# Retention attention and a multiplicative FFN: the first weight quarter in Strassen order, a new order of loads, and q of units 0 and 1 scaled by VectorE

**Chip, cores, metric.** One core of one Trainium2 chip. The metric is the device time of the slowest (here the only) core, in microseconds (us). The kernels of one round ran on the same chip.

## The reference

```python
scores = q @ k.T / sqrt(64);  D[i, j] = gamma_h ** (i - j) for i >= j, else 0
x = ((scores * D) @ v), heads side by side        # 8 batches x 576 tokens, 8 heads x 64 -> 4608 x 512
a = x @ w1;  b = x @ w2                           # 512 x 1024 each
out = ((a * b) @ w3) @ w_out                      # 1024 x 1024, 1024 x 512
```

q, k, v are float32. The weights come as float64 and are read as pairs of 32-bit words; the kernel turns them into float32 itself.

## The kernel before

It works in units of up to 128 positions of two batches (unit 0 has 64). In a unit TensorE transposes k and q, makes scores and a running state, and forms x ("pv"). The products with w1 and w2 ("up") use Strassen's scheme, seven products for eight, one quarter of the features at a time. A weight block of 128 x 512 pairs is converted by VectorE and ScalarE: VectorE cuts out exponent and mantissa (`begin_block`), ScalarE clamps the exponent in two steps, VectorE joins them (`end_block`). The head of the program interleaves all this by hand. Every engine follows its own instructions in the order written here.

```python
    def strassen_weights(fp):
        tt("S1", "A21", "A22", ALU.add)
        tt("S2", "S1", "A11", ALU.subtract)
        yield
        tt("S3", "A11", "A21", ALU.subtract)
        tt("S4", "A12", "S2", ALU.subtract)
        live["S", fp] = True
        yield
...
    def conversion():            # a generator; convert(n) takes n of its steps, convert_up_to(n) ends n blocks
        yield from begin_block()
        while converted[0] < len(blocks):
            if begun[0] < len(blocks) and converted[0] not in (1, 2, 3):
                yield from begin_block()      # the next block is begun before this one is ended
            yield from end_block()
            if begun[0] == converted[0] < len(blocks):
                yield from begin_block()
...
        c = ffn.tile([P, 4, 2, TB], F32, tag="c", name="c", bufs=1)       # in up(), one quarter
        p1 = product(None, "A11", "B11")
        nc.scalar.copy(c[:, 0], p1)
        if first:
            product(p1, "A12", "B21")          # adds into the same bank: waits for the copy
            aside.pop(0)()
        plus(product(None, "S2", "T2"), 1, 0)  # plus: an addition on VectorE and two conversion steps
        plus(product(None, "S3", "T3"), 2, 1)
...
    load_block()                 # the head of the program; load(unit, what)
    load(0, "v")
    load_block()
    load(1, "kq")
    load_block()
    load(1, "v")
    load_block()
    scale(0, "q")                # GpSimd
    front(0, "k"); keep_busy(4); front(0, "q")      # transposes; idle products that keep TensorE at work
    convert(3)
    score(0); scale(0, "v"); state(0)
    convert_up_to(1)
    pv(0)
    load(2, "kqv"); load_block(); load_block()
    convert_up_to(2)
    load_block()
    scale(1, "q")                # GpSimd
    front(1, "k"); keep_busy(6); front(1, "q")
    convert(3)
    scale(1, "v"); score(1); state(1)
    convert_up_to(3); load_block(); convert_up_to(4)
    first_sums = strassen_weights(0); next(first_sums)
    pv(1)
    ...
    up(0, 0, 0, conv=2, tail=False, first=True)
```

## Time and profile before

| | before |
|---|---|
| time, median of 5 runs | 859.64 us (858.93 to 861.71) |
| span of the profiled run | 857.7 us |
| TensorE (PE) / VectorE (DVE) / ScalarE (ACT) / GpSimd (POOL) busy | 98 / 56 / 21 / 14 % |
| first up product starts | 30.57 us |
| TensorE gapless from unit 3's q on | 49.58 to 94 us |

The lines behind these numbers stand in the prediction. One view is added: the chain of work that ended last begins, followed back, in the middle of the head (columns: start us, us, what).

```profile
49.54 0.04 issue
49.58 1.09 PE tp L237 x8
```

What happens before 49.54 counts only as far as it moves that point or one after it.

### The profile page before, as it was taken

The page shows a single profiled execution, that of the slowest core. Times are in us where ns is not written, and L with a number is a line of the kernel's source. Part 1 is how long each engine was busy: PE and PEld are TensorE (multiplying, and loading weights), DVE is VectorE, ACT ScalarE, POOL GpSimd, SP SyncE. Part 2 cuts the span into 40 slices and gives each one's busy share as a digit, 9 for nine tenths or more (in the row PEclk, how much of TensorE's full clock was granted, in tenths as well). Part 3 has the DMA queues.
Part 4 walks back from the last instruction along what each step waited for, and adds up shares of the span by engine and source line. Part 5 has one row for each costly group of instructions (what it writes and reads, how often), then busy time and mean ns, then how long its engine had stood idle before and what let it go on. Part 6 is the DMA issues. An engine that isn't in the chain of part 4 may idle for free.

```text
span 857.7 us, 15368 instructions
## 1 busy us (share of the span) xinstructions
PE 844.7 (98%) x6293; PEld 770.5 (90%) x6293; DVE 482.6 (56%) x797; ACT 179.1 (21%) x358; POOL 119.7 (14%) x96
## 2 busy tenths in 40 slices
PE   8989999999999999999999999999999999999998
PEld 7889999644888999999999999999999999999996
DVE  4899998996744444454544544544454434335343
ACT  3666343342121111010111010111010201001000
POOL 3010020001212213221221130203030101000000
PEclk9999999999999999999999999999999999999999
DMA  9994453454246525352542171534140000000001
GB/s 195 218 225 114 100 96 103 114 156 70 42 98 125 98 34 87 62 109 47 87 86 38 27 122 31 95 65 60 31 69 25 2 25 1 26 25 1 25 1 50
DMA packets 213879, 64.01 MB, mean 75 GB/s; under 512 B 195752, under 2 KB 204200, under 8 KB 213808
## 3 DMA queue, kind: packets, MB, share of 16 engines
q1 hardware_dynamic: 167376, 43.33, 26.4%
q10 hardware_dynamic: 46432, 19.70, 10.3%
q8 instruction: 49, 0.80, 0.4%
q14 instruction: 22, 0.18, 0.1%
HBM read 53.55 MB, written 9.44 MB: 73 GB/s over the span
## 4 chain that ended last, share of the span: by engine, by line
PE 88%; DVE 4%; issue 1%; ACT 1%; DMA 0%; ACTq 0%; DVEq 0%
PE up L506 46%; PE po L617 25%; PE ps L461 6%; PE xps L309 4%; PE sc L252 4%; PE xps L302 2%; PE st L274 1%; DVE c L511 1%; PE tp L237 1%; DMA out_dram<-ot 0%; DVE e L400 0%; ACT e L389 0%; DVE w L411 0%; DVE ab L537 0%; DVE wS L169 0%
## 5 line engine op out<-in xcount | busy, mean ns | idle before, releaser
L511 DVE TENSOR_TENSOR c<-up,c 128x384 f32<-128x384 f32 x240 | 132.5, 552 | 175.2 <-PE up L506 170.9
L506 PE MATMUL up<-xT,wA 128*128 128x192 f32 x1152 | 212.5, 328 | 0.6 <-ACT c L519 0.6
L506 PEld LDWEIGHTS up<-xT,wA 128*128 128x128 f32 x1152 | 190.5, 190 | 3.9 <-ACT c L519 0.9
L506 PE MATMUL up<-T,wS 128*128 128x192 f32 x768 | 140.6, 326 | 0.0
L506 PEld LDWEIGHTS up<-T,wS 128*128 128x128 f32 x768 | 127.4, 190 | 0.2 <-issue 0.2
L617 PE MATMUL po<-w3o,ab 128*128 128x256 f32 x456 | 104.0, 380 | 0.3 <-ACT ot L639 0.3
L617 PEld LDWEIGHTS po<-w3o,ab 128*128 128x128 f32 x456 | 86.0, 190 | 12.1 <-ACT ot L639 0.7
L621 DVE TENSOR_TENSOR ot<-po,ot 128x256 f32<-128x256 f32 x90 | 38.0, 423 | 69.5 <-PE po L617 66.6
L506 PE MATMUL up<-xT,wS 128*128 128x192 f32 x384 | 70.6, 327 | 0.6 <-DVE c L511 0.5
L255 DVE TENSOR_TENSOR pm<-sc,mask 128x512 f32<-128x512 f32 (+1 forms) x80 | 45.4, 627 | 45.4 <-PE sc L252 45.4
L506 PE MATMUL up<-T,wA 128*128 128x192 f32 x384 | 70.2, 326 | 0.0
L531 ACT COPY c<-up 128x384 f32<-128x384 f32 x48 | 22.9, 478 | 226.0 <-PE up L506 224.1
L223 POOL TENSOR_TENSOR ld_v<-ld_v,gk 128x1024 f32<-128x1024 f32 (+1 forms) x17 | 34.5, 2030 | 242.3 <-DMA ld_v<-in_v_dram 179.6
L617 PE MATMUL po<-wB,forms 128*128 128x256 f32 x288 | 65.3, 379 | 0.0
L506 PEld LDWEIGHTS up<-xT,wS 128*128 128x128 f32 x384 | 63.6, 190 | 1.4 <-DVE c L511 1.4
L506 PEld LDWEIGHTS up<-T,wA 128*128 128x128 f32 x384 | 63.7, 190 | 0.0
L617 PEld LDWEIGHTS po<-wB,forms 128*128 128x128 f32 x288 | 54.6, 190 | 7.7 <-issue 0.3
L461 PE MATMUL ps<-wo,w3T 128*128 128x512 f32 x128 | 55.4, 593 | 1.3 <-DVE w3T L415 1.3
L461 PEld LDWEIGHTS ps<-wo,w3T 128*128 128x128 f32 x128 | 23.9, 190 | 32.2 <-issue 30.5
L537 DVE TENSOR_TENSOR ab<-c 128x768 f32<-128x768 f32 x48 | 48.4, 1009 | 4.0 <-DVE c L511 0.5
L519 ACT COPY c<-up 128x384 f32<-128x384 f32 x48 | 22.9, 477 | 120.4 <-PE up L506 70.9
L480 POOL TENSOR_TENSOR T<-xT,T 128x384 f32<-128x384 f32 x20 | 21.5, 1073 | 163.9 <-PE up L506 162.1
(77 smaller groups left out, 818.0 us busy)
## 6 DMA issues: line engine op xcount, KB each, us to landing
raw<-in_moe_w_dram SPq DMA_DIRECT2D x64, 128.0 KB, 3.0
bl_q<-in_q_dram SPq DMA_DIRECT2D x208, 32.0 KB, 2.4
out_dram<-ot ACTq DMA_DIRECT2D x23, 256.0 KB, 2.0
bl_k<-in_k_dram SPq DMA_DIRECT2D x176, 32.0 KB, 2.2
ld_v<-in_v_dram ACTq DMA_DIRECT2D x10, 512.0 KB, 5.9
raw<-in_moe_w_dram SPq DMA_DIRECT2D x8, 512.0 KB, 7.2
raw<-in_moe_w_dram SPq DMA_DIRECT2D x16, 256.0 KB, 5.8
raw<-in_moe_w_out_dram SPq DMA_DIRECT2D x32, 128.0 KB, 2.8
```

The costliest lines, as they stand in the source:

```text
L223: nc.gpsimd.tensor_tensor(out=t, in0=t, in1=gam[:sz, c].unsqueeze(1).unsqueeze(3).to_broadcast([sz, 2, H, D]), op=ALU.mult)
L252: nc.tensor.matmul(sc[j][:sz, p, :sz], kT[hs, b, p, :sz], qT[hs, b, p, :sz], start=True, stop=True)
L255: nc.vector.tensor_mul(pm[:sz, b, j, :, :sz], sc[j][:sz, :, :sz], mask[:sz, :sz].unsqueeze(1).to_broadcast([sz, NP, sz]))
L309: nc.tensor.matmul(banks[r][heads[half], b, n, :sz], vs[:sz, b * H + 2 * p + j, :], pm[:sz, b, j, p, :sz], start=(c == 0 and m == 0), stop ...
L461: nc.tensor.matmul(ps, live["w3T", ft][:, g, :], live["wo"][:, g, :], start=(g == 0), stop=(g == KF - 1))
L506: nc.tensor.matmul(ps[:, w, :], a[:, w, r, :], b[:, r, :], start=(new and w == r == 0), stop=(w == r == 1), skip_group_check=True)
L511: nc.vector.tensor_add(c[:, to], ps, c[:, sb])
L519: nc.scalar.copy(c[:, 0], p1)
L531: nc.scalar.copy(c[:, 0], p1)
L537: nc.vector.tensor_mul(ab[:, 4 * fp:4 * fp + 4, :], c[:, :, 0, :], c[:, :, 1, :])
L617: nc.tensor.matmul(ps[nm], a[A][:, f, :], live["W"][B][:, f, :], start=(f == 0 and not on), stop=(f == NP - 1), skip_group_check=True)
L621: nc.vector.tensor_add(ot[:, to[0], to[1]], ps[nm], ot[:, sb[0], sb[1]])
```

## The change

Intent: let the first up products start sooner. The first quarter's weights come in the order A11, A12, A21, A22, so that the first two products need two blocks, not four; the sums begin with S3 and T3, which need the fewest blocks; unit 1's k and q are loaded ahead of block 1; GpSimd's slower scale of q goes to VectorE for units 0 and 1; the decays go ahead of q in ScalarE's queue. The idle products between unit 1's k and q transposes are taken out. Its core, cut:

```diff
+    dq = ...; nc.scalar.dma_start(dq, decay_q)       # moved up, ahead of load(0, "q", nc.scalar)
@@ strassen_weights, all four quarters
-        tt("S1", "A21", "A22", ALU.add)
-        tt("S2", "S1", "A11", ALU.subtract)
+        tt("S3", "A11", "A21", ALU.subtract)
         yield
-        tt("S3", "A11", "A21", ALU.subtract)
+        tt("S2", "A22", "S3", ALU.subtract)
+        yield
+        tt("S1", "S2", "A11", ALU.add)
         tt("S4", "A12", "S2", ALU.subtract)
@@ blocks
-    blocks = []
-    for fp in range(NQ):
+    blocks = [(("A", r, f), None) for f in range(2) for r in range(2)]   # both matrices in one block
+    for fp in range(1, NQ):
@@ up
             product(p1, "A12", "B21")
             aside.pop(0)()
+            p7 = product(None, "S3", "T3")
         plus(product(None, "S2", "T2"), 1, 0)
-        plus(product(None, "S3", "T3"), 2, 1)
+        plus(p7 if first else product(None, "S3", "T3"), 2, 1)
@@ head of the program
     load_block()
     load(0, "v")
-    load_block()
     load(1, "kq")
     load_block()
     load(1, "v")
     load_block()
-    scale(0, "q")
+    load_block()
+    scale(0, "q", engine=nc.vector)
...
     state(0)
+    front(1, "k")
     convert_up_to(1)
     pv(0)
...
-    convert_up_to(2)
-    load_block()
-    scale(1, "q")
-    front(1, "k")
-    keep_busy(6)
+    scale(1, "q", engine=nc.vector)
     front(1, "q")
...
+    weight_sums = strassen_weights(0)                # S3
+    next(weight_sums)
     pv(1)
...
+    token_sums = strassen_tokens(0, 0, nc.vector)    # T3, T2
+    next(token_sums)
+    convert_up_to(4)
+    next(weight_sums)                                # S2
+    list(token_sums)                                 # T1, -T4
+    list(weight_sums)                                # S1, S4
```

More of the change, by code (lines that the diff above doesn't have):

```diff
@@ L115, in load @@
             live[nm, g] = t
+    dq = ffn.tile([P, 4, 2, TB], F32, tag="c", name="dq", bufs=1).rearrange("p a b s -> p (a b s)")[:H, :S]
+    nc.scalar.dma_start(dq, decay_q)
     load(0, "k")
@@ L132 @@
     gqs = const.tile([P, NP, S // 32], F32, tag="gqs", name="gqs")
-    dq = ffn.tile([P, 4, 2, TB], F32, tag="c", name="dq", bufs=1).rearrange("p a b s -> p (a b s)")[:H, :S]
-    nc.scalar.dma_start(dq, decay_q)
     nc.scalar.dma_start(gk[:short, 0, :], decay_k[:short, :])
@@ L155 @@
     halves = range(DF // CV)
-    wA = [wp.tile([P, 2, KD, CV], F32, tag=f"wA{h}", name="wA") for h in halves]
+    wA = [wp.tile([P, 2, 2, KD // 2, CV], F32, tag=f"wA{h}", name="wA") for h in halves]
     wS = [wp.tile([P, 3, 2, 2, 2, P], F32, tag=f"wS{h}", name="wS") for h in halves]
@@ L164, in A @@
         r, f = {"A11": (0, 0), "A12": (1, 0), "A21": (0, 1), "S3": (0, 1), "A22": (1, 1)}[nm]
-        return wA[h][:, :, 2 * r:2 * r + 2, m * QC + f * P:m * QC + f * P + P]
+        return wA[h][:, r, :, :, m * QC + f * P:m * QC + f * P + P]
     def strassen_weights(fp):
@@ L212, in front_blocks, with scale @@
             live[nm + "T", g] = dst
-    def scale(g, nm, scalar=False):
+    def scale(g, nm, scalar=False, engine=nc.gpsimd):
         c = g % NC
@@ L222, in scale @@
             return
-        nc.gpsimd.tensor_tensor(
+        engine.tensor_tensor(
             out=t, in0=t, in1=gam[:sz, c].unsqueeze(1).unsqueeze(3).to_broadcast([sz, 2, H, D]), op=ALU.mult)
@@ L335, in load_block @@
         t = raw.tile([P, CV, 2], I32, tag="raw", name="raw", bufs=5)
-        if key[0] == "w12":
-            _, fp, _, r = key
-            src = w[2 * r * P:2 * (r + 1) * P, fp * QC:(fp + 1) * QC, :]
-            t2 = t.rearrange("p (c n) t -> p c n t", c=2)
-            if r == 0:
-                nc.sync.dma_start(t2, src.rearrange("(c p) n t -> p c n t", p=P))
-            else:
-                for half in range(2):
-                    nc.sync.dma_start(t2[heads[half]],
-                                      src.rearrange("(c a d) n t -> a d c n t", a=2, d=D)[1 - half])
+        if key[0] in ("A", "w12"):
+            if key[0] == "A":
+                _, r, f = key
+                t4 = t.rearrange("p (j c n) t -> p j c n t", j=2, c=2)
+                parts = [(t4[:, j], w[:, f * P:(f + 1) * P]) for j, w in enumerate((moe_w1, moe_w2))]
+            else:
+                _, fp, _, r = key
+                parts = [(t.rearrange("p (c n) t -> p c n t", c=2), w[:, fp * QC:(fp + 1) * QC])]
+            for t2, src in parts:
+                src = src[2 * r * P:2 * (r + 1) * P]
+                if r == 0:
+                    nc.sync.dma_start(t2, src.rearrange("(c p) n t -> p c n t", p=P))
+                else:
+                    for half in range(2):
+                        nc.sync.dma_start(t2[heads[half]],
+                                          src.rearrange("(c a d) n t -> a d c n t", a=2, d=D)[1 - half])
         elif key[0] == "wo":
@@ L359, in converted_to @@
         key, _ = blocks[n]
+        if key[0] == "A":
+            return A(0, {(0, 0): "A11", (1, 0): "A12", (0, 1): "A21", (1, 1): "A22"}[key[1:]]).rearrange(
+                "p j c n -> p (j c) n")
         if key[0] == "w12":
             _, fp, j, r = key
-            return wA[fp // 2][:, j, 2 * r:2 * r + 2, fp % 2 * QC:fp % 2 * QC + QC]
+            return wA[fp // 2][:, r, j, :, fp % 2 * QC:fp % 2 * QC + QC]
         if key[0] == "wo":
@@ L403, in end_block @@
         key = blocks[n][0]
-        while not (key[0] == "w12" or "wo" in live and (key[0] == "wo" or key[1] < multiplied[0] + 3)):
+        while not (key[0] in ("A", "w12") or "wo" in live and (key[0] == "wo" or key[1] < multiplied[0] + 3)):
             yield "wait"
         out, m, e = converted_to(n), m.bitcast(F32), e.bitcast(F32)
+        if key[0] == "A":
+            m, e = (x.rearrange("p (c n) -> p c n", c=4) for x in (m, e))
         if key[0] == "w12":
@@ L421, in end_block @@
             load_block()
-        if key[0] == "w12" and key[1] > 0 and key[2:] == (1, 1):
+        if key[0] == "w12" and key[2:] == (1, 1):
             yield from strassen_weights(key[1])
@@ L477, in strassen_tokens, with tt @@
             [P, 2, TB], F32, tag="T", name="T", bufs=1 if m == 1 and j == 2 else 5) for j in range(3)]
-        def minus(out, in0, in1):
-            engine.tensor_tensor(out=out, in0=in0, in1=in1, op=ALU.subtract)
+        def tt(out, in0, in1, op=ALU.subtract):
+            engine.tensor_tensor(out=out, in0=in0, in1=in1, op=op)
         live["B", i, n] = {"B11": B[0][0], "B21": B[1][0], "B22": B[1][1], "T3": B[0][1],
                            "T1": T[0], "T2": T[1], "-T4": T[2]}
-        minus(T[0], B[0][1], B[0][0])
-        minus(T[1], B[1][1], T[0])
-        minus(B[0][1], B[1][1], B[0][1])
-        minus(T[2], B[1][0], T[1])
+        tt(B[0][1], B[1][1], B[0][1])
+        tt(T[1], B[0][1], B[0][0], ALU.add)
+        yield
+        tt(T[0], B[1][1], T[1])
+        tt(T[2], B[1][0], T[1])
+        yield
     def up(i, n, fp, conv=0, tail=True, first=False):
@@ L493, in up @@
         if ("B", i, n) not in live:
-            strassen_tokens(i, n)
+            list(strassen_tokens(i, n))
         if fp == 0:
@@ L535, in up @@
         if fp == NQ - 1 and m + 1 < len(every) and has_x(*every[m + 1]) and ("B", *every[m + 1]) not in live:
-            strassen_tokens(*every[m + 1])
+            list(strassen_tokens(*every[m + 1]))
         nc.vector.tensor_mul(ab[:, 4 * fp:4 * fp + 4, :], c[:, :, 0, :], c[:, :, 1, :])
@@ L697 @@
     state(1)
+    convert_up_to(2)
+    load_block()
+    convert(4)
     convert_up_to(3)
     load_block()
-    convert_up_to(4)
-    first_sums = strassen_weights(0)
-    next(first_sums)
+    weight_sums = strassen_weights(0)
+    next(weight_sums)
     pv(1)
@@ L706 @@
     load_block()
-    strassen_tokens(0, 0, nc.vector)
-    for _ in first_sums:
-        pass
+    token_sums = strassen_tokens(0, 0, nc.vector)
[4 more added lines that the diff above has]
+    list(weight_sums)
     aside.append(lambda: scale(2, "q", True))
@@ L732 @@
     pv(3)
-    strassen_tokens(0, 1, nc.vector)
+    list(strassen_tokens(0, 1, nc.vector))
     score(4)
@@ L871 @@
         if g == NC + 1:
-            strassen_tokens(1, 0)
+            list(strassen_tokens(1, 0))
             todo.extend((up, 1, 0, fp) for fp in range(NQ))
```

## The prediction

> **What bounds the kernel now.** I read the page first. TensorE is busy almost everywhere, so a change in the head of the program pays only as far as it lets TensorE go on earlier, and its idle time caps the gain.
>
> ```profile
> PE 844.7 (98%) x6293; PEld 770.5 (90%) x6293; DVE 482.6 (56%) x797; ACT 179.1 (21%) x358; POOL 119.7 (14%) x96
> PE   8989999999999999999999999999999999999998
> ```
>
> The span is 857.7 us, so PE is idle for 13.0 us in all. The view of waits, for PE alone, says where the named part lies:
>
> ```profile
> PE tp L237 <- POOL ld_q L223: 2.1, 1, 2.1
> PE gps L142 <- DMA dq<-decay_q_dram: 2.1, 1, 2.1
> PE ps L461 <- DVE w3T L415: 1.3, 1, 1.3
> PE up L506 <- ACT c L519: 0.6, 1, 0.6
> ```
>
> Only the first of these, and the last, lie where the change works and can carry to the end. Next I read the timeline of PE, from the second unit's transposes to the second feature quarter (columns: start us, duration us, engine, line, operation):
>
> ```profile
> 18.24 1.97 PE L237 MATMUL tp<-ident,ld_k 128*128 128x128 f32 x8
> 20.00 2.09 PE L151 MATMUL idle<-ident 128*128 128x128 f32 x12
> 21.92 1.04 PE L237 MATMUL tp<-ident,ld_q 128*128 128x128 f32 x8
> 30.57 1.57 PE L506 MATMUL up<-xT,wA 128*128 128x192 f32 x8
> 49.58 1.09 PE L237 MATMUL tp<-ident,ld_q 128*128 128x128 f32 x8 [2.13 <-POOL ld_q L223]
> 57.85 1.46 PE L506 MATMUL up<-T,wS 128*128 128x192 f32 x8
> ```
>
> The reader is to see that the first up product starts at 30.57, that PE fills its wait with idle products at 20.00, and that at 49.58 it stood 2.13 us for the q of unit 3. From there to 94 us PE is gapless. The chain that ended last starts at that very place, so nothing before it counts by itself. GpSimd's timeline says what held that q:
>
> ```profile
> 17.47 1.97 POOL L223 TENSOR_TENSOR ld_q<-ld_q,gq 128x1024 f32<-128x1024 f32 x1 [3.64 <-DMA ld_q<-in_q_dram]
> 47.31 2.21 POOL L223 TENSOR_TENSOR ld_q<-ld_q,gq 128x1024 f32<-128x1024 f32 x1 [22.01 <-DVE pm L255]
> ```
>
> The second is put down to VectorE, but its issue stands at 34.05 in the queue and the longest landing of a q load is 13.1 us: 34.05 + 13.1 = 47.15, so it was the transfer. Lastly VectorE's timeline:
>
> ```profile
> 17.71 2.27 DVE L411 SCALAR_TENSOR_TENSOR wA<-m,e 128x512 f32<-128x512 f32 x1
> 36.14 0.55 DVE L511 TENSOR_TENSOR c<-up,c 128x384 f32<-128x384 f32 x1
> 56.54 0.69 DVE L169 TENSOR_TENSOR wS<-wS,wA 128x512 f32<-128x512 f32 x1
> ```
>
> VectorE runs without a gap from the first addition of a product (36.14) to the sum S2 of the second quarter (done 57.23), 21.1 us of work. PE takes that S2 at 57.85. So there are two gates into the gapless stretch: the q of unit 3 (49.58, no slack) and this S2 (0.6 us of slack).
>
> **What the Trainium skill says.** "SBUF — State Buffer", section "Who interferes with whom": VectorE with two inputs in SBUF and GpSimd reading SBUF hold a shared pair of ports in turn, and the second blocks. The trace agrees: three conversion steps beside a GpSimd scale took 2.27 us where they take 0.69, ending some 0.5 us after it. "VectorE: DVE Perf Modes", section "Why `tensor_tensor` can't do 2×_2P or 4×": fp32 products of two tensors run at one element a cycle; the trace has 512 elements in 0.69 us and 768 in 0.95, so 1024 cost an estimated 1.2 us. "TensorE: Matmul & The Clock Gate", part 1: the array runs at half rate until some 3.4 us of sustained work and after an idle window of that size. The trace agrees on the factor: eight k transposes took 1.97 us at 18.24, eight q ones 1.04 at 21.92, after the filler. "DMA: Bandwidth & Descriptors", section "Why small descriptors are slow": each packet has a fixed overhead. Weight runs of 1 KB replace 2 KB here.
>
> **The change part by part.** (1) The decays move ahead of q on ScalarE's queue. This removes the 2.1 us wait for dq and brings unit 0's scores some 2 us forward, but unit 1 gates what follows, so I count nothing.
>
> (2) The first weight block now holds A11 of both matrices, then A12, A21, A22, so the first two up products need two blocks, not four. Twelve DMAs of half the run take the place of six. The bytes are the same. If the shorter runs cost 5 to 10%, 2 MB at some 290 GB/s become 0.4 to 0.7 us longer.
>
> (3) The k and q of unit 1 go ahead of block 1. They land an estimated 2.5 us sooner (0.5 MB at 210 GB/s), near 15. But the order of instructions shows that VectorE scales this q only after the start of block 1's conversion, which waits for block 1. The bytes up to there (k, q, v of unit 0, k and q of unit 1, two blocks) are just those that before had landed at 17.47. From 17.2: three conversion steps 1.4, the end of block 0's conversion 1.3, the scale 1.2, so q is ready at 21.1; before, PE took it at 21.92. The gain is 0.8 us, not 2.5. From here the same work as before (8.65 us from 21.92 to 30.57) puts the first up product near 29.9.
>
> (4) The filler of six idle products goes (2.1 us), but it filled a wait that stays: after pv of unit 0, near 16, PE has nothing until 21.1.
>
> (5) Two scales go from GpSimd to VectorE: 2 x 1.2 us are added, and two of the three 1.58 us stalls go. In part they come back: unit 1's v now lands near 20, so that GpSimd's scale (1.91 us) meets VectorE's conversion instead of its mask products out of PSUM, which did not suffer.
>
> (6) The sums in the new order. S2 now needs S3, which needs block 2, then block 3. In ScalarE's queue the two exponent steps of block 3 (1.5 us) now stand ahead of the copy of the first product, and PE's second product waits for that copy. VectorE begins block 3 only after T3 and T2, which need the copied x of unit 1 (near 30.4): T3 and T2 until 31.4, exponent step 31.8, two ScalarE steps to 33.3, copy to 33.8. So the second product starts at 33.8 against 32.70 before, the third, S3 T3, follows at 35.1, S2 T2 at 36.4, and is done at 37.7. The first addition to its result then starts near 37.8, against 36.14.
>
> (7) The same 21.1 us from there, VectorE's order up to the second quarter's S2 being unchanged in its operations, make S2 ready at 58.9; PE wanted it at 57.85. That is 1.0 us later, plus or minus 1 for the landing of block 1. The gate of q3 stays: the same bytes stand ahead of it in the same order. A dip of the transfer rate near 20 us (153 and 192 GB/s against some 210) may be filled, about 0.5 us of gain, eaten by the shorter runs.
>
> (8) After 60 us the products are the same. One more step per weight quarter in the conversion shifts three VectorE slots; with 1.8 us of named PE waits after that (0.5 on c, 1.3 on w3T), I allow 0.5 us either way.
>
> The sum: +1.0 (the S2 gate), 0 (the q3 gate), 0 (rest). I take half of the first off, since the landing of block 1 is my weakest figure and an earlier one gives it back one for one: +0.5 us, 860.1 us.
>
> **The rivals.** First, the head does get shorter. If block 1 lands 1.5 us earlier than I think, and the fill of the dip moves q3 too, both gates open sooner: 1 to 2.5 us of gain, 857 to 858.5. For it: the queue no longer stalls on q's landing (its second block was held from 2.94 to 7.6). Against it: the transfer rate was near 210 GB/s all that time, so nothing was starved. Second, the array turns cold. PE stands some 5 us before unit 1's q transposes with no filler; if a whole idle window falls in, the 7.3 us of unit 1's attention on PE run at half rate for some 3.5 us or more, and the first up product comes 2 to 4 us later. That is 862 to 864. For it: the 2:1 rates seen around 20 us. Against it: the new head works PE without a break from 1.4 to some 10 us, and the gap may be just short enough. Third, the whole difference is hidden behind q3: the time is the same to 0.3 us, 859.4 to 860. For it: the 2.13 us that PE stands there swallow any delay of that size on PE's own path; against it, the S2 gate passes it by.
>
> **Range and chances.** The gates allow a gain of at most some 2.5 us (the wait of 2.1, half a us of ScalarE wait), and the cold array costs up to 4; I give the hidden case or the small loss half of the chances, the gain 0.3, the cold array 0.2. Eight in ten: 857.2 to 863.2. Two per cent are 17 us, more than all of PE's idle time, so faster by that is out of reach; slower by that would need a new wait in every round, and nothing repeated has changed but the order of four sums. Faster 0.01, same 0.98, slower 0.01.
>
> **What would show each step.** Right: VectorE's scale of unit 1's q starts between 19 and 20.5, not at q's landing near 15; the first up product between 29 and 31; PE waiting over 1 us for ScalarE's copy of the first product; the first addition near 37.8; unit 3's q still scaled at 47 to 48; no conversion step of 2.27 us before 20. Cold: k transposes or scores of unit 1 at twice the time. Wrong: PE gapless from 30 to 41, the S2 of the second quarter before 57, or unit 3's q by 45; then the time is 857 or below. Also wrong if the time moves and the stretch up to 60 us did not: then the order of the sums, or the conversion's extra step, matters later.

## The result, and the profile after

The changed kernel takes 869.29 us (median of 5, 868.56 to 871.02) against 859.64. A ratio here is the mean time of one kernel's fast runs over that of the other's of the same rounds, so not quite the ratio of the quoted medians: 1.0113, 95% interval 1.0094 to 1.0131. It is slower by 9.7 us, where the prediction had 0.5.

TensorE's waits, for PE alone (engine, line, waited for: us in total, times, longest):

```profile
PE tp L238 <- issue: 4.9, 1, 4.9
PE ps L474 <- DVE w3T L428: 2.5, 2, 1.8
PE up L521 <- ACT c L534: 2.2, 1, 2.2
PE up L521 <- DVE wS L169: 1.7, 1, 1.7
```

The old wait of 2.1 us for unit 3's q is gone, and four others stand in its place. The first is put to "issue" by the profile; the timelines show what it was. TensorE's (same places as in the prediction):

```profile
15.52 1.97 PE L238 MATMUL tp<-ident,ld_k 128*128 128x128 f32 x8
24.31 1.94 PE L238 MATMUL tp<-ident,ld_q 128*128 128x128 f32 x8 [4.93 <-issue]
26.18 3.79 PE L253 MATMUL sc<-qT,kT 64*128 64x128 f32 x32
35.10 1.47 PE L521 MATMUL up<-xT,wA 128*128 128x192 f32 x8
38.76 2.87 PE L521 MATMUL up<-xT,wA 128*128 128x192 f32 x16 [2.19 <-ACT c L534]
53.83 1.04 PE L238 MATMUL tp<-ident,ld_q 128*128 128x128 f32 x8
64.08 1.54 PE L521 MATMUL up<-T,wS 128*128 128x192 f32 x8 [1.66 <-DVE wS L169]
```

VectorE's and GpSimd's:

```profile
18.55 0.43 DVE L390 TENSOR_SCALAR e<-raw 128x512 int32<-128x512 int32 x1 [5.32 <-DMA raw<-in_moe_w_dram]
21.29 2.92 DVE L224 TENSOR_TENSOR ld_q<-ld_q,gq 128x1024 f32<-128x1024 f32 x1
43.03 0.56 DVE L526 TENSOR_TENSOR c<-up,c 128x384 f32<-128x384 f32 x1 [0.37 <-PE up L521]
```

```profile
20.84 2.29 POOL L224 TENSOR_TENSOR ld_v<-ld_v,gk 128x1024 f32<-128x1024 f32 x1 [7.29 <-DMA ld_v<-in_v_dram]
47.73 2.28 POOL L224 TENSOR_TENSOR ld_q<-ld_q,gq 128x1024 f32<-128x1024 f32 x1 [24.60 <-DVE c L526]
```

Read in time: VectorE waits 5.32 us for block 1 (18.55), ends block 0, and only then comes to the scale of q (21.29), which takes 2.92 us where it had 1.2 to do, because GpSimd began its scale of v at 20.84. TensorE, whose last product ended near 19.4, gets q at 24.31. Its clock is at half by then. This is the table by stretches (us, busy PE, PEld, DVE, ACT, POOL, then the granted clock, the DMA share and GB/s) of the changed kernel:

```profile
8.00:18.00 10.00, 7.62 (x94) 6.61 (x94) 4.08 (x8) 3.74 (x7) 1.90 (x1) 0.59 1.14 189
24.00:30.00 6.00, 5.69 (x42) 5.16 (x44) 3.13 (x6) 1.17 (x2) 0.00 (x0) 0.50 1.34 214
30.00:36.00 6.00, 6.00 (x110) 5.59 (x111) 4.92 (x9) 3.00 (x5) 0.00 (x0) 0.97 1.12 253
```

So unit 1's transposes and scores took 1.94 and 3.79 us where they had 1.04 and 2.06. From the up product at 35.10 to the first addition at 43.03 it is 7.93 us, against 5.57 before. Unit 3's q, scaled at 47.73, is no longer waited for (53.83). That scale meets a conversion step of VectorE, as it did before the change (2.27 us where the step takes 0.69):

```profile
48.29 2.27 DVE L424 SCALAR_TENSOR_TENSOR wA<-m,e 128x512 f32<-128x512 f32 x1
```

Two landmarks split the loss: the start of S2 T2 in the second quarter, 57.85 us before and 64.08 after (+6.2), and from there to the end, 799.85 and 802.42 us (+2.6). The sum is the 8.8 us between the profiled spans. The 6.2 us of the head, against the kernel before, are: q taken 2.4 us later, 2.1 us more from q to the first up product, 2.4 us more from there to the first addition, less 0.2 us in VectorE's stretch to S2 (20.9 instead of 21.1) and 0.5 us of slack that S2 had (57.23 to 57.85 before, 63.93 to 64.08 now).

### The profile page after: what moved, and what is told of

Read it like the earlier page. It is cut to its first block, busy times and chain, and to the rows that moved or that the text cites.

```text
span 866.5 us, 15333 instructions
## 1 busy us (share of the span) xinstructions
PE 845.0 (98%) x6281; PEld 769.8 (89%) x6281; DVE 484.4 (56%) x799; ACT 179.1 (21%) x358; POOL 111.9 (13%) x94
## 4 chain that ended last, share of the span: by engine, by line
PE 90%; DVE 5%; issue 2%; DMA 1%; ACT 0%; SPq 0%; POOL 0%; ACTq 0%; DVEq 0%; POOLq 0%
PE up L521 49%; PE po L633 24%; PE ps L474 6%; PE sc L253 4%; PE xps L310 4%; PE xps L303 2%; PE st L275 2%; DMA ld_v<-in_v_dram 1%; PE tp L238 1%; DVE c L526 1%; DVE e L411 1%; DMA out_dram<-ot 0%; DVE m L397 0%; DVE ab L553 0%; DVE forms L603 0%
```

## The experiments

**Theory** after reading the traces: the loss has two parts. In the head, the scale of unit 1's q stands on VectorE behind the start of block 1, which the new order of loads makes late; the gap cools TensorE (this part did not hold, see e1), GpSimd's scale of v collides, and the late copy adds to it. Later, the third conversion step per quarter costs time. **Rivals**: VectorE's conversion gates the first 58 us, so nothing on TensorE or in the order of q matters; or the order of loads is bad by itself; or the half clock is all of it.

Landmarks from each profiled run, in us ("edit on" is the kernel that was edited; "b1" is VectorE's start on block 1; "q" is TensorE's start on unit 1's q transposes; "rest" is from S2 T2 of the second quarter to the end):

| run | edit on | b1 | q | first up | first addition | S2 T2 | rest | time, median | ratio to before |
|---|---|---|---|---|---|---|---|---|---|
| before | | 15.60 | 21.92 | 30.57 | 36.14 | 57.85 | 799.85 | 859.64 | |
| changed | | 18.55 | 24.31 | 35.10 | 43.03 | 64.08 | 802.42 | 869.29 | 1.0113 |
| e1 filler | changed | 18.92 | 24.55 | 32.85 | 42.46 | 63.38 | 802.22 | 867.39 | 1.0095 |
| e2 v on ScalarE | changed | 19.58 | 23.63 | 33.89 | 43.50 | 64.57 | 801.43 | 867.49 | 1.0093 |
| e3 scale ahead | changed | 19.04 | 18.37 | 31.60 | 39.52 | 58.98 | 802.52 | 864.45 | 1.0073 |
| e4 two steps | changed | 18.02 | 23.78 | 34.15 | 43.77 | 64.86 | 800.94 | 868.79 | 1.0110 |
| e5 copy ahead | changed | 19.08 | 24.71 | 35.21 | 42.80 | 63.53 | 802.47 | 867.99 | 1.0093 |
| e6 no filler | before | 15.48 | 20.10 | 30.66 | 35.66 | 60.58 | 800.52 | 861.98 | 1.0017 |
| e7 k, q sooner | before | 17.43 | 21.84 | 31.83 | 37.40 | 57.85 | 801.05 | 860.23 | 1.0006 |
| e8 old order | changed | 13.29 | 20.41 | 30.43 | 38.36 | 57.83 | 802.47 | 863.24 | 1.0045 |
| e9 = e8 + e4 | changed | 13.45 | 19.34 | 30.39 | 39.97 | 61.14 | 800.96 | 863.29 | 1.0041 |
| e10 = e9 + e5 | changed | 12.87 | 20.08 | 30.91 | 38.50 | 58.19 | 801.01 | 861.19 | 1.0019 |
| e11 unit 3's q | before | 15.84 | 22.62 | 31.28 | 36.85 | 57.65 | 799.95 | 859.30 | 0.9994 |
| e12 all mends | changed | 13.84 | 20.74 | 30.44 | 38.03 | 58.65 | 801.25 | 860.93 | 1.0017 |
| e13 = e1 + e5 | changed | 18.91 | 24.58 | 32.87 | 40.47 | 61.18 | 802.02 | 865.75 | 1.0068 |
| e14 q on GpSimd | changed | 18.88 | 18.38 | 30.79 | 38.73 | 58.19 | 802.31 | 862.25 | 1.0032 |

All gave the right result. The intervals of the ratios are about 0.0012 to 0.003 on either side. The kernel before ran in every round, the changed kernel in the first alone (the rounds of the edits were on four chips), so between rounds the ratio is to be compared, not the median. A landmark is from one profiled execution.

### e14: unit 1's q back on GpSimd

```diff
-    scale(1, "q", engine=nc.vector)
+    scale(1, "q")
```

> The changed kernel with unit 1's q scaled by GpSimd as before, nothing else. Theory (the gap comes from the scale standing behind block 1's conversion on VectorE; GpSimd takes it when q lands, near 15.5): the q transposes start at 18.5 to 19.5, the first up product near 31, S2 T2 of the second quarter near 59, 4 to 6 us off: 863 to 865, as the run that moved the scale ahead on VectorE. Rival (the stall of the ports makes GpSimd's scale as dear): the transposes start after 21 and under 2 us come off.

Measured: 862.25 us, ratio 1.0032 (1.0005 to 1.0059). GpSimd's timeline and TensorE's in this run:

```profile
15.49 1.90 POOL L224 TENSOR_TENSOR ld_q<-ld_q,gq 128x1024 f32<-128x1024 f32 x1 [2.87 <-DMA ld_q<-in_q_dram]
```

```profile
18.38 1.97 PE L238 MATMUL tp<-ident,ld_q 128*128 128x128 f32 x8
30.79 1.47 PE L521 MATMUL up<-xT,wA 128*128 128x192 f32 x8
```

q had landed by 15.49, while the changed kernel scaled it at 21.29. This one line undone moves S2 T2 from 64.08 to 58.19: 5.9 of the 6.2 us of the head. It is the largest single cause. Not all of it is the wait for q, though. The first addition comes 4.3 us sooner (38.73). The other 1.6 us are a port stall (VectorE held up beside GpSimd) that falls away: GpSimd's scale of unit 3's q now meets unit 2's mask products, which take their usual time, and not a conversion step:

```profile
46.83 2.23 POOL L224 TENSOR_TENSOR ld_q<-ld_q,gq 128x1024 f32<-128x1024 f32 x1 [24.09 <-PE sc L253]
47.21 2.48 DVE L256 TENSOR_TENSOR pm<-sc,mask 128x512 f32<-128x512 f32 x4
```

VectorE's stretch from the first addition to S2 is 19.3 us here, where the changed kernel has 20.9. The same holds in e3 and e8 (19.3 each).

### e3: the same scale on VectorE, moved ahead of block 1's conversion

```diff
     front(1, "k")
+    scale(1, "q", engine=nc.vector)
     convert_up_to(1)
...
-    scale(1, "q", engine=nc.vector)
```

> The changed kernel with VectorE's scale of unit 1's q moved in program order ahead of block 1's conversion. Theory (the gap is made by the order on VectorE, which waits 5.3 us for block 1 with q already landed): q is scaled by 17 to 18, the q transposes follow pv of unit 0 at 19.4 without a gap, the first up product starts near 30 and 4 to 6 us come off: 863 to 865 us. Rival (q itself lands late, near 20): the transposes start only after 21 and less than 3 us come off.

Measured: 864.45 us (863.50 to 868.17). VectorE scales q at 15.48 in 1.23 us, TensorE's transposes follow at 18.37, S2 T2 starts at 58.98 (5.1 us sooner, of which 3.5 at the first addition). The first up product came at 31.60 and not near 30: the scores waited 1.71 us for ScalarE's copy of the transposed q and then ran at half rate (3.79 us). So it is not the engine but the place in its order: a wait for block 1 stood ahead of work whose data had been there for 3 us.

### e8: block 1 ahead of unit 1's k and q again

```diff
     load(0, "v")
+    load_block()
     load(1, "kq")
     load_block()
     load(1, "v")
     load_block()
-    load_block()
```

> The changed kernel with weight block 1 loaded ahead of unit 1's k and q, as before; all else as changed. Theory (block 1's late landing starves VectorE, 5.3 us of waiting for it): VectorE begins block 1 near 15.6, scales unit 1's q by 19.5, the 4.9 us gap of TensorE falls under 1 us, the first up product starts near 31.5 and 3 to 5 us come off: 864 to 866. Rival (the gap follows from VectorE having to scale q at all): the q transposes still start after 22.

Measured: 863.24 us, ratio 1.0045. Block 1 is begun at 13.29, so VectorE comes to q in time (19.08, 1.23 us), and S2 T2 starts at 57.83, where the kernel before has it. Undoing either half, the order of loads or the place of the scale, gives S2 T2 back. The first addition is still 2.2 us later than in the kernel before (38.36 against 36.14); the port stall that fell away pays for most of that.

### e7: the new order of loads alone, in the kernel before

```diff
     load(0, "v")
-    load_block()
     load(1, "kq")
     load_block()
     load(1, "v")
     load_block()
+    load_block()
```

> The kernel before with unit 1's k and q loaded ahead of weight block 1, nothing else. Theory (VectorE's conversion is the bound of the first 58 us, and a later block 1 starves it): VectorE begins block 1 near 18.5 instead of 15.6, the first up addition starts 1.5 to 3 us after 36.14, and the total is 1 to 2.5 us above before. Rival (the order of loads is good, the other parts lose): unit 1's scores come 2 us sooner and the total is at or under before.

Measured: 860.23 us, ratio 1.0006 (0.9991 to 1.0022): the same. My theory here was wrong in its size, and the rival in its reason: unit 1's scores came at 23.12, no sooner than before (23.19). The first addition did come 1.26 us later (37.40), as a block 1 begun at 17.43 asks. But S2 T2 stayed at 57.85: GpSimd's scale of unit 3's q met the mask products for part of its time, VectorE's stretch up to S2 was 0.8 us shorter (20.3 instead of 21.1), and S2's slack took the rest. The order of loads is harmless by itself; the loss of the head needs it together with the scale on VectorE.

### e1 and e13: the half clock

```diff
     scale(1, "q", engine=nc.vector)
+    keep_busy(11)
     front(1, "q")
```

> The changed kernel with eleven idle products put back on TensorE in the 4.9 us gap before unit 1's q transposes. Theory (the array is at half rate because the gap and the two short ones before it let it cool): the eight q transposes take 1.04 us instead of 1.94 and the 32 score products 2.06 instead of 3.79, the first up product starts near 32.6 instead of 35.1, and 2.2 to 2.6 us come off the total: some 867 us where the changed kernel has 869.3. Rival (VectorE's conversion gates the first quarter anyhow): the transposes are fast but the first up addition stays at 43.0 and the total at 869.

Measured: 867.39 us. As the theory said, transposes (1.06) and scores (2.06) ran at full rate and the first up product started at 32.85, 2.25 us sooner. But the first addition moved by 0.6 us only. In the table by stretches of this run there is a second spell of half clock, and TensorE's timeline shows it behind the wait for the copy:

```profile
24.00:36.00 12.00, 9.52 (x152) 8.49 (x152) 10.06 (x18) 5.43 (x10) 0.00 (x0) 1.00 1.09 229
38.00:40.00 2.00, 2.00 (x8) 2.00 (x7) 2.00 (x5) 2.00 (x8) 0.00 (x0) 0.50 1.18 189
```

```profile
36.51 4.55 PE L521 MATMUL up<-xT,wA 128*128 128x192 f32 x16 [2.19 <-ACT c L534]
```

Sixteen matmuls took 4.55 us where the profiled run of the changed kernel has 2.87. Of the eight profiled runs with this wait of 2.2 us, four show such a spell (e1, e2, e4 and e9, 4.3 to 4.6 us), and the changed kernel, e3, e8 and e14 do not (2.87).

The theory is right about the filler and wrong about the gap. The array was at half rate before the gap began: the k transposes at 15.52 took 1.97 us, and the clock of 8 to 18 us is 0.59. In e3 and e14, where q follows without the gap, the 32 scores take 3.79 us all the same. In the kernel before, the k transposes are slow too (1.97) and only the q transposes, behind the idle products of `keep_busy(6)`, are fast (1.04). The change took these products out.

So e13 took both away, the half clock of unit 1's attention and (by e5's edit, below) the wait for the copy.

> The changed kernel with eleven idle products in the gap before unit 1's q transposes and with the first product and its copy ahead of block 3's conversion. Theory (half clock and the late copy are separate losses of 2 us each, and the one hid the other): the first up product near 32.8, no clock under full after 25 us, the first up addition near 40, S2 T2 of the second quarter near 61, and 3 to 4 us off: some 866. Rival (VectorE's own work gates S2 whatever TensorE does): the first addition stays over 42 and under 2 us come off.

Measured: 865.75 us, ratio 1.0068; first addition at 40.47, S2 T2 at 61.18. Compared with e5, which lacks only the filler (S2 T2 at 63.53), the half clock in unit 1's attention is worth 2.3 us. The rival that VectorE hides all of this falls, and so does the one that the half clock is all of the loss: 2.3 of 6.2 us.

### e5: the copy ahead of block 3's exponent steps

The first product, its copy and the second product are issued ahead of `convert_up_to(4)`; the rest of `up` follows as it was.

```diff
     next(token_sums)
+    begun_up = up(0, 0, 0, first="begin")      # A11 B11, the copy, A12 B21
     convert_up_to(4)
...
-    up(0, 0, 0, conv=2, tail=False, first=True)
+    up(0, 0, 0, conv=2, tail=False, first=begun_up)
```

> The changed kernel with the first up product, its copy and the second product issued ahead of block 3's conversion, so that the copy stands before block 3's exponent steps in ScalarE's queue. Theory (the copy waits 2.2 us behind those steps, and this wait is new): the 2.2 us wait of TensorE for the copy falls to 0.6, S2 T2 follows VectorE's S2 at once, 1.2 to 1.6 us come off at the second quarter's S2 and the total is some 867 to 868; the second spell of half clock near 37 us, which some runs show, goes too. Rival (VectorE's sums gate S2 T2 anyway): the wait moves to the sums and the first up addition still starts near 43.

Measured: 867.99 us. The wait for the copy fell from 2.2 to 0.6 us, but TensorE then waited 0.8 us for S2 and the first addition came only 0.2 us sooner (42.80). The rival holds mostly: behind the copy, VectorE's sums were nearly as late. Of the 0.55 us at S2 T2, 0.2 are this and 0.3 a shorter port stall in VectorE's stretch to S2 (20.6 instead of 20.9). The time lies in the theory's 867 to 868, but the intervals of the two ratios overlap (1.0077 to 1.0108 here, 1.0094 to 1.0131 for the changed kernel), so a gain of 1.3 us is not shown.

### e2: unit 1's v scaled by ScalarE

```diff
-    scale(1, "v")
+    scale(1, "v", True)
```

> The changed kernel with unit 1's v scaled by ScalarE, not GpSimd. Theory (GpSimd's scale of v holds the shared ports while VectorE wants to scale q): the q scale takes 1.2 us instead of 2.92, the q transposes start near 22.6 instead of 24.3, still at half rate, and 1.7 us come off the total: some 867.6 us. Rival (the long q scale has another cause, as a broadcast operand): it stays near 2.9 us.

Measured: 867.49 us. The scale of q took 1.22 us instead of 2.92: the collision is shown. In e1, e5 and e13, where GpSimd scales v at the same time but VectorE comes to q later, the stall falls on a conversion step instead (2.27 to 2.31), and q takes 1.21.

```profile
22.31 1.22 DVE L224 TENSOR_TENSOR ld_q<-ld_q,gq 128x1024 f32<-128x1024 f32 x1
```

The first up product came 1.2 us sooner (33.89), though block 1 was begun 1.0 us later in this run. The first addition did not: in the profiled run the second spell of half clock took 4.40 us for the sixteen matmuls. The timed gain, 1.8 us, agrees with the theory, but S2 T2 shows none (64.57) and the interval (1.0076 to 1.0109) overlaps that of the changed kernel, so what the collision costs in the end is not shown.

### e4: the weight sums of quarters 1 to 3 in two steps

```diff
         tt("S3", "A11", "A21", ALU.subtract)
-        yield
+        if fp == 0:
+            yield
         tt("S2", "A22", "S3", ALU.subtract)
```

> The changed kernel with the weight sums of quarters 1 to 3 in two conversion steps as before, not three. Of the 9 us lost, 6.3 are lost by 91 us and 2.5 after, of which 1.2 at the first two w3 products. Theory (the extra steps push the conversion later): the waits for w3T fall from 2.5 to some 1.3 us and 0.5 to 1.5 us come off, 868 us. Rival (the late waits follow from the head's delay of VectorE): nothing changes, 869.3 within 0.5.

Measured: 868.79 us, 0.5 below. TensorE's wait for the transposed w3 is that of the kernel before again:

```profile
PE ps L475 <- DVE w3T L429: 1.3, 1, 1.3
```

The "rest" fell from 802.42 to 800.94, 1.5 us, and in this profiled run the head happened to be 0.8 us later (64.86). All runs with three steps lie between 801.4 and 802.5, all edits of the changed kernel with two between 800.9 and 801.3. So the step costs about 1.2 us by the traces, and the wait for w3 agrees (2.5 us with three steps, 1.3 with two, in every profiled run). The times do not show it: 0.5 us here, and nothing between e8 and e9, which differ in this step (863.24 and 863.29); in both pairs the head of the profiled runs differs too.

### e9, e10, e12: the mends together

e9 is e8 with e4; e10 adds e5.

> The changed kernel with block 1 loaded ahead of unit 1's k and q and with the sums of quarters 1 to 3 in two steps: the two undone parts that each gave something. Theory (the head's loss and the later loss are separate and add): 3.1 us above before less 1.5 us for the steps, so 1 to 2.5 us above before, near 862; w3T waits of 1.3 us, the second quarter's S2 T2 near 57.8. Rival (the later waits follow the head, so once the head is right the steps do nothing): as the run with the old order alone, 3 to 4 us above before.

> As the last, and with the first product, its copy and the second product ahead of block 3's conversion. Theory (with the order of loads right, the wait for the copy is the next bound): the 2.2 us wait of TensorE falls to 0.6, the first up addition starts near 37, S2 T2 of the second quarter near 57 or at what unit 3's q allows, and 0.5 to 1 us more come off: within 1 us of before. Rival (unit 3's q is the gate by now): TensorE waits for GpSimd's scale of it instead and nothing comes off.

Measured: e9 863.29 us with runs from 860.31 to 865.50, 3.9 us above that round's 859.41. That is the rival's number, but not for its reason: the wait for w3 is 1.3 us and the rest 800.96, as the theory said, while S2 T2 came at 61.14, because the profiled run had half clock from 34 to 37 us behind the wait for the copy. e10, without that wait, 861.19 us (1.0006 to 1.0031), 1.8 us above and not within 1: the first addition came at 38.50, not near 37, S2 T2 at 58.19, and TensorE waits 0.32 us for GpSimd's scale of unit 3's q. e12 adds two idle products ahead of unit 1's q transposes and scales unit 3's q on VectorE, right after unit 2's mask products:

```diff
-    scale(3, "q")
     convert(1)
...
     front(3, "k")
+    scale(3, "q", engine=nc.vector)
     convert(2)
```

> The changed kernel with all four mends (old order of loads, two steps, copy ahead, two idle products before unit 1's q transposes) and unit 3's q scaled by VectorE. Theory (the mends add): S2 T2 of the second quarter at 56 to 57, 0.5 to 1.5 us under before. Rival (the transfers bound the way to unit 3's q, whatever else is done): TensorE waits for that q until 48.5 or later and the time is that of before within 0.5 us.

Measured: 860.93 us, ratio 1.0017 (1.0005 to 1.0029), 1.5 us above. Unit 3's q transposes start at 50.21 and S2 T2 at 58.65. The theory missed. The rival, that the transfers bound the way there, does not explain it either: q was issued at 34.2 and landed 12.7 us later, near 46.9, and VectorE came to it at 48.90 straight from the mask products. The two idle products were too few (the q transposes took 1.91 us). With these faults mended the new head is no better than the old one: in no run with the new head did the first up product start before 30.39 (30.57 in the kernel before), and the first addition is still 1.9 us later (38.03 against 36.14). The new order of blocks and sums was not run by itself.

### e11: unit 3's q on VectorE, in the kernel before

The edit is the one just shown, on the kernel before.

> The kernel before with unit 3's q scaled by VectorE right after the mask products of unit 2, instead of by GpSimd. Theory (two gates lead into the gapless stretch, unit 3's q and VectorE's S2; this eases both: 1.2 us of scale in place of 2.2, and one 1.6 us port stall of VectorE gone): the q transposes of unit 3 start near 48.6 instead of 49.6, S2 T2 of the second quarter near 56.9, 0.5 to 1 us under before. Rival (VectorE stands in its order until q lands, 47.3, and loses what it gains): the same as before within 0.3 us.

Measured: 859.30 us, ratio 0.9994 (0.9982 to 1.0006). The transposes start at 49.11 instead of 49.58, and S2 T2 at 57.65 instead of 57.85: no gain that counts. The rival's number holds, not its reason: VectorE came to q straight from the mask products (47.80), later than q's landing near 46.1 (issued at 33.9, 12.2 us to landing). In this profiled run the first addition was 0.7 us later (36.85), so how far the gates moved is not settled. No version was found that beats the kernel before.

### e6: the kernel before without its filler

```diff
-    keep_busy(6)
```

> The kernel before with its six idle products ahead of unit 1's q transposes taken out, nothing else. Theory (the filler keeps or makes the array fast): the q transposes start at 20.0 instead of 21.9 but at half rate (1.94 us), the scores take 3.7 instead of 2.06, and the first up product starts 0.5 to 2 us later than 30.57; the total is 0.5 to 2 us above before. Rival (the filler only costs time): the first up product starts up to 1.9 us earlier, at 28.7, and the total is the same or less.

Measured: 861.98 us (859.76 to 862.81), interval 0.9995 to 1.0040: unclear, with most runs 1 to 3 us above. Transposes (1.97) and the first scores ran at half rate, but the first up product started at 30.66, only 0.1 us later, since the idle time saved paid for it. What this profiled run lost, it lost at unit 3's q: a wait of 3.29 us, after which eight transposes took 1.89 us instead of 1.09.

## Why the prediction was wrong

**What bounds the kernel** was right: two gates lead out of the head, and the S2 gate decided. From the first addition to S2 the text gave 21.1 us; the changed trace has 43.03 to 63.93, 20.9 us. That it fits is in part luck: the stretch holds one port stall of 1.6 us, which depends on where GpSimd's scale of unit 3's q happens to fall, and without it (e3, e8, e14) it is 19.3 us. The scale of unit 3's q stayed where it was (47.73 against 47.31).

**Step (3)** failed in size. It had q ready at 21.1; TensorE took it at 24.31. Block 1 was begun at 18.55 instead of 17.2 (1.35 us of the miss). The new order of loads alone, with the old weight blocks, begins it at 17.43 (e7), so most of that goes with the other changes to the loads. Step (2)'s smaller DMAs are the likely ones, but no run isolates them; their 0.4 to 0.7 us (at 290 GB/s, where step (3) takes 210) were not carried into this sum. The collision, which step (5) saw coming ("unit 1's v now lands near 20"), made the scale 1.7 us longer and was not put into the sum. That VectorE scales q only after block 1 was seen before the run and judged a gain of 0.8 us. It is the cause that e14 and e3 show, worth 5 to 6 us with what follows from it.

**Step (4)** failed: it took the idle products for a mere filling of a wait. They also brought the array to full rate, and the change leaves unit 1's attention at half rate without them: 24.31 to 35.10 took 10.8 us instead of the 8.65 the text carried over. e13 against e5 makes it 2.3 us. This is the cold array, a rival with 0.2, though not by its gap (see e1). The rival was kept apart from the sum, as if only one of the stories could come true. They add on one chain: +3.2 for q, +2.1 for the clock.

**Step (6)** was right: from the first up product to the first addition it gave 7.9 us (29.9 to 37.8), and 7.93 were measured, with the predicted wait for ScalarE's copy (2.2 us). e5 adds that the sums behind it were nearly as late, so mending the copy alone gives little.

**Step (8)** was short. It allowed 0.5 us for the extra conversion step and all that comes late; 2.6 were measured. The step itself is some 1.2 to 1.5 us (e4). The remaining 1.1 us stay open: e7 and e6, which have the old sums, also show a rest of 801.05 and 800.52 where the kernel before has 799.85, so it is not clearly the change's.

**The order of loads**, step (3)'s 2.5 us, I took for a small good; e7 shows it is worth nothing in the kernel before, and e8 that it is needed for the loss at S2 T2.

A note on the prediction's reading of the skill: that fp32 products of two tensors stay at the single rate is stated in that page's section on mode 2×_2P; the section named there gives the reason.

The sum by its terms, in profiled spans: predicted +1.0 at the S2 gate (+0.5 after halving) and 0 later; measured +6.2 and +2.6.

## What to carry to other kernels

An engine follows its order, so an operation moved to it waits for everything written ahead of it: look at what that work waits for, not only at how long the operation takes. An earlier load that cost nothing by itself (e7) and a scale on a faster engine that cost nothing at S2 T2 with the old loads (e8) moved that point by 6 us together. When an early point moves, see also which operations of two engines now meet: the same scale of GpSimd cost VectorE 1.6 us in one run and nothing in the next. Idle products before a wait are part of the schedule, and delays that fall on one chain are added, not weighed against each other.

## What the Trainium skill lacked or had wrong

- "TensorE: Matmul & The Clock Gate", section "HAM oscillation — how this bites in real kernels": it gives gaps over some 3.4 us as what cools the array. Here 2.19 us were enough in e1 (16 matmuls in 4.55 us instead of 2.87, clock 0.50 from 38 to 40 us), while the same wait left the changed kernel's profiled run at full clock (2.87 us); four of eight profiled runs with it slowed. In the changed kernel the clock fell near 10 us, after products of 64 x 64 and gaps of 1.2 us or less.
- Same page, part 1: it counts the warm-up as some 3.4 us of sustained work. The kernel before worked without a gap from 8.2 to 18.2 us, mostly in 64-wide products, and its next eight transposes still took 1.97 us instead of 1.04; only 128-wide work after them brought the full rate, by 21.9.
- Same page, part 1: it warns that a trace's clock events can be unreliable, but does not name this case. Here the granted clock read 1.00 over stretches at half rate: e3 has 1.00 in every stretch from 0 to 50 us, with scores of 3.79 us at 22.05. The durations told it, not the column.
- "SBUF — State Buffer", section "Who interferes with whom": agrees, but gives no size for these operations; here it is 2.92 us for a VectorE scale of 1.22 (e2), with GpSimd's side at 2.29 instead of 1.90.
- "DMA: Bandwidth & Descriptors" names a fixed overhead per packet but has no measured rate for runs of 1 KB against 2 KB in trn2's HBM loads. With the same bytes ahead of it, block 1 was begun at 17.43 us with 2 KB runs (e7) and at 18.0 to 19.6 with twice as many DMAs of 1 KB runs (all runs with the changed loads). The runs do not tell the packet size from the number of DMAs.
